# Order and queue assignment of the first loads in a gated mix of linear attention and a GEGLU feed-forward block

## The chip, the cores and the metric

The kernel runs on one core of one Trainium2 chip. The metric is the device time of one execution in microseconds (us); the number compared is the median over several executions of the same program. A profiled execution also has a span, the time from its first to its last instruction.

## The reference

All tensors are bf16; S = 2048 rows, D = 640 columns, F = 1728 hidden columns, 32 heads of 20.

```python
x = A_x                                                 # (1, 2048, 640)
g = sigmoid((x * gate_w).sum(-1, keepdims=True))
q, k, v = split_heads(x @ A_wqkv)                       # A_wqkv (640, 1920)
phi = lambda t: where(t > 0, t + 1, exp(t)) + 1e-6
kv, z = einsum("bhsd,bhse->bhde", phi(k), v), phi(k).sum(s)
o = einsum("bhqd,bhde->bhqe", phi(q), kv) / (einsum("bhqd,bhd->bhq", phi(q), z) + 1e-6)
a = merge_heads(o) @ A_wo
b = (gelu(x @ B_w_gate) * (x @ B_w_up)) @ B_w_down
out = g * a + (1 - g) * b
```

## The kernel before

The program is one long list of operations for five engines. Each operation is recorded by a helper, `P.op`, with the buffers that it reads and writes; from these the helper derives the semaphore waits. Nothing reorders the list: each engine runs its operations in the order in which the source records them, and each DMA queue (SP's, issued by SyncE, and ACT's, issued by ScalarE) gets its loads in that order too. Every load has a semaphore of its own, so whoever needs one chunk waits for that chunk alone.

The 2048 rows are 16 tiles of 128 rows, and the 640 columns of x are 5 chunks of 128 (index k). The work on TensorE goes through these stages, in this order:

1. The start. `warm(count, n)` (line 417) issues matmuls on constants, whose results nobody reads. `T(i, ks, tb)` (line 431) transposes the chunks `ks` of x tile i on TensorE into PSUM bank `tb`, and VectorE copies the result into `xT` (line 435): one copy for chunk 0, one for chunks 1 to 4. This is done for the x tiles 0 and 1 only. `KM(n, [k])` (lines 451 and 452) multiplies chunk k of x tile n by chunk k of the K weights `wk`, 512 and 128 columns, and accumulates over k. `gate_col` puts `gate_w` into column 640 of the Q weights. `QM` (lines 466 and 467) does for the Q weights `wq` what `KM` does for `wk`.
2. `KQ(i)` (line 536) does both products for the x tiles 2 to 15. Their transposed form comes by DMA transposes (line 373) that SP issues; the first of them waits for `wk` chunk 4. ScalarE and VectorE form phi from PSUM (lines 476 to 490, 546 to 555).
3. The products phi(k) with x (lines 593 to 608), the two hidden products of the feed-forward block (line 697), in which the attention's small matrices are formed as well, and the output products (lines 808 to 861).

The first loads, each of 160 KB (128 rows of 640 bf16) apart from two small ones, are recorded in this order; `load_x(i)` loads x tile i, `load_wk(k)` and `load_wq(k)` load the 128 rows of chunk k of the K and of the Q weights:

| Queue | Loads in order |
|---|---|
| SP | x tile 0, wk 0, wk 1, wk 3, wq 0, wq 2, wq 4, then the transposes |
| ACT | touch load, x tile 1, wk 2, wk 4, gate_w (1.2 KB), wq 1, wq 3 |

The touch load (line 355) reads 16 pieces of 8 bytes from the K weights into a buffer that nothing reads. Between x tile 1 and wk 2, ScalarE also has an exp on a constant (line 364), before which its table is loaded.

The start of TensorE's list reads:

```python
warm(5, 512)
warm(1, 128)
T(0, [0], 7)
T(0, [1, 2, 3, 4], 6)
warm(6, 128)
KM(0, [0])
T(1, [0], 7)
T(1, [1, 2, 3, 4], 6)
warm(3, 128)
KM(1, [0])
for k in (1, 2, 3):
    KM(0, [k])
    KM(1, [k])
gate_col()
```

Of the kernel before, what the change touches and what calls it, by code (L numbers as in the profile page):

```python
# [161 lines left out]
def bass_gated_mix__linear_attn_block__geglu_ffn__prompt_kernel(  # L162
# [63 lines left out]
    with (  # L226
# [8 lines left out]
        with contextlib.ExitStack() as stack:  # L235
            dma_sems = [stack.enter_context(nc.semaphore("s_in%d" % i)) for i in range(n_dma_in)]

            P = _Plan(["pe", "act", "dve", "pool", "sp"])
# [9 lines left out]
            def new_dma_key():  # L248
                k = "in%d" % dma_next[0]
                dma_next[0] += 1  # L250
                return k

            def v16(o, n):
                return pool[:, o:o + n]
# [46 lines left out]
            touch = v16(O_TOUCH, 16)  # L301
# [37 lines left out]
            def dma_in(dst, src, writes, reads=(), eng="sp"):  # L339
                P.op(eng, lambda e, dst=dst, src=src: e.dma_start(dst, src),  # L340
                     reads=reads, writes=writes, dma=new_dma_key())
# [3 lines left out]
            def load_x(i, eng="sp"):  # L345
                dma_in(x_aug[:, i, 0:640], A_x[0, i * 128:(i + 1) * 128, :], [r_xn[i]], eng=eng)

            def load_wk(k, eng="sp"):
                dma_in(wk[:, k, :], A_wqkv[k * 128:(k + 1) * 128, 640:1280], [r_wk[k]], eng=eng)

            def load_wq(k, eng="sp"):
                dma_in(wq[:, k, 0:640], A_wqkv[k * 128:(k + 1) * 128, 0:640], [r_wq[k]], eng=eng)


            P.op("act", lambda e: e.dma_start(touch[0:16, 0:4], A_wqkv[0:128:8, 640:644]),
                 writes=[P.res("touch")], dma=new_dma_key())
            load_x(0)
            load_wk(0)
            load_x(1, "act")
            load_wk(1)  # L360
            load_wk(3)

            zero = nc.const_aps.tensor(0.0, (128, 1), F32)
            P.op("act", lambda e: e.activation(eg[:, 0:1], zero, ACT.Exp), writes=[r_eg[0]])
            load_wk(2, "act")
            load_wk(4, "act")
            P.op("dve", lambda e: e.memset(gw_sb, 0.0), writes=[r_gw])
            dma_in(gw_sb[0:5, :], gate_w.rearrange("(k p) -> k p", p=128), [r_gw], eng="act")
            for k in range(KC):
                load_wq(k, ("sp", "act")[k % 2])  # L370

            def load_xT(i, after=()):
                P.op("sp", lambda e: e.dma_start_transpose(xT[:, :, i * 128:(i + 1) * 128],
# [39 lines left out]
            def warm(count, n):  # L413
                def fn(e):
                    last = None
                    for w in range(count):
                        last = e.matmul(ps[:, 4, 0:n], one_l, one_r[:, 0:n], start=True, stop=True)
                    return last
                P.op("pe", fn, writes=[bank[4]])
# [4 lines left out]
            def slot(n):  # L424
                return SLOTS[n % 4]

            def T(i, ks, tb):
                def fn(e):
                    last = None
                    for n, k in enumerate(ks):  # L430
                        last = e.transpose(psb[:, tb, n * 128:(n + 1) * 128],
                                           x_aug[:, i, k * 128:(k + 1) * 128], ident)
                    return last
                P.op("pe", fn, reads=[r_xn[i], r_ident], writes=[bank[tb]])
                P.op("dve", lambda e: e.tensor_copy(
                    xT[:, ks[0]:ks[-1] + 1, i * 128:(i + 1) * 128],
                    psb[:, tb, 0:len(ks) * 128].rearrange("p (k s) -> p k s", k=len(ks))),
                    reads=[bank[tb]], writes=[r_xTa[i] if ks[0] == 0 else r_xT[i]])
# [4 lines left out]
            def KM(n, ks):  # L443
                i = seq[n][1]
                b0, b1 = slot(n)

                def fn(e):
                    last = None
                    for k in ks:
                        lhs = xT[:, k, i * 128:(i + 1) * 128]  # L450
                        e.matmul(ps[:, b0, :], lhs, wk[:, k, 0:512], start=(k == 0), stop=(k == KC - 1))  # L451
                        last = e.matmul(ps[:, b1, 0:128], lhs, wk[:, k, 512:640],
                                        start=(k == 0), stop=(k == KC - 1))
                    return last
                P.op("pe", fn, reads=[r_xTa[i] if i < NXN and ks == [0] else r_xT[i]] + [r_wk[k] for k in ks],
                     writes=[bank[b0], bank[b1]])
# [51 lines left out]
            KM(0, [0])  # L508
            T(1, [0], 7)
            T(1, [1, 2, 3, 4], 6)  # L510
            warm(3, 128)
            KM(1, [0])
            for k in (1, 2, 3):
                KM(0, [k])
                KM(1, [k])
            gate_col()
# [409 lines left out]
```

## Time and profile before

| What | Value |
|---|---|
| Median of 5 runs | 274.27 us (273.56 to 274.69) |
| The profiled execution | 274.07 us, its span 272.8 us |
| TensorE matmuls (PE) | busy 268.6 us, 98% of the span |
| VectorE (DVE) | busy 141.8 us, 52% |
| ScalarE (ACT) | busy 76.0 us, 28% |
| GpSimd (POOL) | busy 30.0 us, 11% |
| DMA | 23.61 MB, 87 GB/s on average |

The engines' busy times overlap, so they don't add up to the span. A matmul's busy time runs from its start until its result has drained, and the next one starts before that; the distance between the starts of two neighbours tells the pace. PEld is the load of the stationary operand. SPq and ACTq are the sequencers of SyncE and ScalarE when they issue a DMA; "us to landing" is the time from the issue until the last piece has arrived and the semaphore is full.

### The profile page before, as it was taken

The page shows a single profiled execution, that of the slowest core. Times are in us where ns is not written, and L with a number is a line of the kernel's source. Part 1 is how long each engine was busy: PE and PEld are TensorE (multiplying, and loading weights), DVE is VectorE, ACT ScalarE, POOL GpSimd, SP SyncE. Part 2 cuts the span into 40 slices and gives each one's busy share as a digit, 9 for nine tenths or more (in the row PEclk, how much of TensorE's full clock was granted, in tenths as well). Part 3 has the DMA queues.
Part 4 walks back from the last instruction along what each step waited for, and adds up shares of the span by engine and source line. Part 5 has one row for each costly group of instructions (what it writes and reads, how often), then busy time and mean ns, then how long its engine had stood idle before and what let it go on. Part 6 is the DMA issues. An engine that isn't in the chain of part 4 may idle for free.

```text
span 272.8 us, 3426 instructions
## 1 busy us (share of the span) xinstructions
PE 268.6 (98%) x1343; PEld 128.8 (47%) x1369; DVE 141.8 (52%) x251; ACT 76.0 (28%) x132; POOL 30.0 (11%) x28
## 2 busy tenths in 40 slices
PE   8999999999999999999999999999999999999997
PEld 4555555544445444444444444444444444444444
DVE  2698988998233335999999999634210000000200
ACT  2455554310422453233222223224011122121021
POOL 5000000003240002242332422000000000000000
DMA  7776999600200011512221221263031110110211
GB/s 224 163 111 123 316 401 388 156 3 16 61 19 2 23 50 50 188 39 48 26 48 24 48 45 30 60 221 103 5 77 38 41 38 19 38 41 19 58 58 41
DMA packets 42208, 23.61 MB, mean 87 GB/s; under 512 B 31567, under 2 KB 40783, under 8 KB 42063
## 3 DMA queue, kind: packets, MB, share of 16 engines
q1 hardware_dynamic: 41429, 22.56, 30.7%
q10 hardware_dynamic: 762, 0.82, 0.9%
q8 instruction: 11, 0.18, 0.3%
q14 instruction: 6, 0.05, 0.1%
HBM read 13.83 MB, written 2.63 MB: 60 GB/s over the span
## 4 chain that ended last, share of the span: by engine, by line
PE 94%; DVE 2%; DMA 2%; issue 1%; ACT 1%; SPq 0%; DVEq 0%; ACTq 0%
PE ps L697 41%; PE ps L861 23%; PE ps L536 12%; PE ps L593 6%; PE ps L840 4%; PE ps L808 2%; DMA pool<-in_A_wqkv_dram 2%; PE ps L675 2%; PE ps L596 2%; PE ps L821 1%; PE ps L451 1%; PE ps L466 1%; DVE pool L490 1%; PE ps L718 1%; DVE pool L555 1%
## 5 line engine op out<-in xcount | busy, mean ns | idle before, releaser
L697 PE MATMUL ps<-pool 128*128 128x512 bf16 x510 | 113.0, 379 | 0.5
L697 PEld LDWEIGHTS ps<-pool 128*128 128x128 bf16 x520 | 50.5, 98 | 60.0
L861 PE MATMUL ps<-pool 128*128 128x512 bf16 (+2 forms) x300 | 62.4, 366 | 0.3
L703 ACT ACTIVATE pool<-ps 128x512 f32<-128x512 f32 x52 | 31.1, 597 | 73.1 <-PE ps L697 73.1
L705 DVE TENSOR_TENSOR pool<-ps,pool 128x512 bf16<-128x512 f32 x52 | 34.7, 689 | 31.7 <-PE ps L697 30.4
L861 PEld LDWEIGHTS ps<-pool 128*128 128x128 bf16 x306 | 29.2, 98 | 33.4 <-issue 0.4
L536 PE MATMUL ps<-pool 128*128 128x512 bf16 (+1 forms) x206 | 37.9, 343 | 0.2
L844 DVE TENSOR_TENSOR pool<-ps,pool 128x512 bf16<-128x512 f32 x4 | 2.8, 692 | 61.5 <-PE ps L840 61.5
L751 POOL TENSOR_TENSOR pool<-pool 128x640 f32<-128x640 bf16 x16 | 22.5, 1407 | 72.8 <-DVE pool L753 65.7
L868 ACT ACTIVATE pool<-ps,pool 128x512 bf16<-128x512 f32 (+1 forms) x16 | 10.9, 681 | 68.6 <-PE ps L861 68.6
L536 PEld LDWEIGHTS ps<-pool 128*128 128x128 bf16 x210 | 20.5, 98 | 17.5
L555 DVE SCALAR_TENSOR_TENSOR pool<-ps,pool 128x128 bf16<-128x128 f32 (+2 forms) x42 | 25.3, 602 | 2.4
L546 ACT ACTIVATE pool<-ps 128x640 bf16<-128x640 f32 x28 | 19.7, 704 | 18.1 <-DVE pool L555 10.6
L593 PE MATMUL ps<-pool 128*128 128x512 bf16 x76 | 19.2, 379 | 0.1
L761 DVE TENSOR_TENSOR pool<-pool 128x640 bf16<-128x640 bf16 x16 | 13.2, 825 | 0.6
L759 DVE TENSOR_SCALAR pool<-pool 128x32 f32<-128x32 f32 x16 | 12.9, 804 | 0.6
L753 DVE TENSOR_REDUCE pool<-pool 128x32 f32<-128x640 f32 x16 | 12.9, 809 | 0.0
L641 DVE TENSOR_TENSOR pool<-pool 128x640 f32<-128x640 f32 x14 | 11.6, 825 | 0.5
L840 PE MATMUL ps<-pool 128*128 128x512 bf16 x51 | 11.5, 379 | 0.1
L643 POOL PARTITION_ALL_REDUCE pool<-pool x1 | 4.0, 3972 | 61.3 <-DVE pool L641 61.3
L593 PEld LDWEIGHTS ps<-pool 128*128 128x128 bf16 x78 | 7.0, 98 | 7.2
L552 DVE TENSOR_SCALAR pool<-pool 128x640 bf16<-128x640 bf16 x28 | 9.1, 327 | 1.8 <-ACT pool L546 0.4
(70 smaller groups left out, 106.4 us busy)
## 6 DMA issues: line engine op xcount, KB each, us to landing
out_dram<-pool SPq DMA_DIRECT2D x19, 128.0 KB, 1.7
pool<-in_B_w_gate_dram SPq DMA_DIRECT2D x1, 2080.0 KB, 14.5
pool<-in_B_w_up_dram SPq DMA_DIRECT2D x1, 2080.0 KB, 19.1
pool<-in_A_x_dram SPq DMA_DIRECT2D x1, 1280.0 KB, 8.7
pool<-in_B_w_down_dram SPq DMA_DIRECT2D x1, 1120.0 KB, 6.1
pool<-omg_row SPq DMA_DIRECT2D x1, 1024.0 KB, 4.6
pool<-in_A_wqkv_dram SPq DMA_DIRECT2D x6, 160.0 KB, 4.7
pool<-in_A_x_dram SPq DMA_DIRECT2D x1, 960.0 KB, 5.5
```

The costliest lines, as they stand in the source:

```text
L536: last = e.matmul(ps[:, b + p, 0:c1 - c0], xT[:, k, i * 128:(i + 1) * 128], wkq[:, k, c0:c1], start=(k == 0), stop=(k == KC - 1))
L546: P.op("act", lambda e: e.activation(e_buf[m], ps_flat[:, o:o + 640], ACT.Exp), reads=banks, writes=[r_e[m]])
L555: P.op("dve", lambda e, c0=c0, c1=c1: e.scalar_tensor_tensor(dst[:, c0:c1], ps_flat[:, o + c0:o + c1], 1.0 + EPS, e_buf[m][:, c0:c1], ALU. ...
L593: last = e.matmul(ps[:, b, :], pk[i][:, c * 128:(c + 1) * 128], x_aug[:, i, 0:512], start=(i == 0), stop=(i == NT - 1))
L697: last = e.matmul(ps[:, b, :], w[:, k, fc * 128:(fc + 1) * 128], xT[:, k, j * 512:(j + 1) * 512], start=(k == 0), stop=(k == KC - 1))
L703: P.op("act", lambda e: e.activation(ge[n], ps[:, gb, :], ACT.Gelu_apprx_tanh), reads=[bank[gb]], writes=[r_ge[n]])
L705: P.op("dve", lambda e: e.tensor_tensor(hT[fc][:, j * 512:(j + 1) * 512], ps[:, ub, :], ge[n], ALU.mult), reads=[bank[ub], r_ge[n]], write ...
L751: P.op("pool", lambda e: e.tensor_tensor(tmp[n], pq[i], z_b, ALU.mult), reads=[r_pq[i], r_zb], writes=[r_tmp[n]])
L753: P.op("dve", lambda e: e.tensor_reduce(den[n], tmp[n].rearrange("p (h d) -> p h d", h=32), AX.X, ALU.add), reads=[r_tmp[n]], writes=[r_de ...
L761: P.op("dve", lambda e: e.tensor_tensor(pq[i].rearrange("p (h d) -> p h d", h=32), pq[i].rearrange("p (h d) -> p h d", h=32), den[n].unsqu ...
L840: last = e.matmul(ps[:, b, :], wd[:, fc, 512:640], hT[fc][:, j * 512:(j + 1) * 512], start=False, stop=(fc == NFC - 2), skip_group_check=True)
L861: last = e.matmul(ps[:, pb, 0:c1 - c0], lhs, rhs, start=False, stop=(q == len(rows) - 1), skip_group_check=True)
```

## The change

The queues' lists become:

| Queue | Loads in order |
|---|---|
| SP | x tile 0, x tile 1, wk 2, wk 4, wq 1, wq 3, then the transposes |
| ACT | wk 0, wk 1, wk 3, gate_w, wq 0, wq 2, wq 4 |

The touch load is dropped. On ScalarE the exp on a constant stands between wk 1 and wk 3. On TensorE, `warm(3, 128)` is dropped, and `KM(0, [1])` stands in its place, ahead of `KM(1, [0])`; `KM(1, [1])` follows it. Nothing else changes on any engine.

```diff
-            P.op("act", lambda e: e.dma_start(touch[0:16, 0:4], A_wqkv[0:128:8, 640:644]),
-                 writes=[P.res("touch")], dma=new_dma_key())
             load_x(0)
-            load_wk(0)
-            load_x(1, "act")
-            load_wk(1)
-            load_wk(3)
+            load_wk(0, "act")
+            load_x(1)
+            load_wk(1, "act")
+            load_wk(2)
+            load_wk(4)
 
             zero = nc.const_aps.tensor(0.0, (128, 1), F32)
             P.op("act", lambda e: e.activation(eg[:, 0:1], zero, ACT.Exp), writes=[r_eg[0]])
-            load_wk(2, "act")
-            load_wk(4, "act")
+            load_wk(3, "act")
             P.op("dve", lambda e: e.memset(gw_sb, 0.0), writes=[r_gw])
             dma_in(gw_sb[0:5, :], gate_w.rearrange("(k p) -> k p", p=128), [r_gw], eng="act")
             for k in range(KC):
-                load_wq(k, ("sp", "act")[k % 2])
+                load_wq(k, ("act", "sp")[k % 2])
...
             T(1, [1, 2, 3, 4], 6)
-            warm(3, 128)
+            KM(0, [1])
             KM(1, [0])
-            for k in (1, 2, 3):
+            KM(1, [1])
+            for k in (2, 3):
                 KM(0, [k])
                 KM(1, [k])
```

## The prediction

> **What bounds the kernel now.** I read the page's busy shares first: TensorE is busy for 98% of the span. The chain of waits, in order of time and up to 12 us, then says what TensorE waits for at the start:
>
> ```profile
> 0.79 0.40 SPq L340
> ...
> 1.26 0.41 SPq L340
> ...
> 1.71 4.31 DMA pool<-in_A_wqkv_dram
> 6.01 0.05 issue
> 6.06 0.39 PE ps L451
> ```
>
> The chain runs through SP's third load, wk 1: issued at 1.71, landed at 6.01 us. `KM(0, [1])` starts 0.05 later, and from there to the last matmul the chain is nearly all TensorE. The neighbours' starts show no pause longer than 0.1 us after 6.06 that isn't one missing matmul record (0.22 us). So the time of the kernel is the moment at which the dense stretch begins, plus a constant. A move of that moment by 0.1 us moves the whole time by 0.1 us.
>
> The timeline from 4.7 to 6.7 us shows what stands just ahead (start, duration, engine, line):
>
> ```profile
> 4.29 0.63 PE L451 MATMUL ps<-pool 128*128 128x512 bf16 x1
> 4.72 0.31 PE L452 MATMUL ps<-pool 128*128 128x128 bf16 x1
> ...
> 4.83 0.69 PE L431 MATMUL ps<-pool 128*128 128x128 bf16 x5
> ...
> 5.35 0.34 PE L417 MATMUL ps<-const-bfloat16-1.0 128*128 128x128 bf16 x3
> ...
> 5.53 0.38 PE L451 MATMUL ps<-pool 128*128 128x512 bf16 x1
> ...
> 5.55 0.42 DVE L435 COPY pool<-ps 128x512 bf16<-128x512 bf16 x1 [0.15 <-PE ps L431]
> 5.74 0.22 PE L452 MATMUL ps<-pool 128*128 128x128 bf16 x1
> 6.06 0.10 PEld L451 LDWEIGHTS ps<-pool 128*128 128x128 bf16 x1 [0.43 <-DMA pool<-in_A_wqkv_dram]
> ```
>
> Two things are to be seen. First, there are 0.18 us of dummies (5.35 to 5.53) and, after the last pair, some 0.26 us of nothing (5.80 to 6.06: at this pace a 128-column matmul takes 0.06). Second, TensorE's pace changes. At 4.29 a 512-column matmul holds the array for 0.43 us (next start 4.72), at 5.53 for 0.21 us: the pace doubles at about 5.3 us, 4.5 us after the first matmul (0.82). The granted clock reads 1.00 in every window of the profile, so here the distances of starts are the evidence, not that column.
>
> The windows say whether the loads are limited by latency or by bandwidth (busy of each engine, then granted clock, DMA share, GB/s):
>
> ```profile
> 0.82:3.14 2.32, 2.31 (x6) 0.70 (x7) 0.11 (x1) 1.42 (x2) 1.96 (x4) 1.00 0.47 129
> 3.14:5.25 2.11, 2.11 (x18) 1.83 (x18) 0.72 (x3) 0.07 (x1) 1.37 (x4) 1.00 1.00 314
> 5.25:6.06 0.81, 0.71 (x8) 0.38 (x7) 0.57 (x2) 0.00 (x0) 0.00 (x0) 1.00 1.05 368
> ```
>
> From 3.14 on the DMA engines are full. With 129 GB/s for 2.32 us and 314 for 2.11, some 960 KB, nearly six loads, have been moved by 5.25, yet only three had landed: the end of wk 1 trails. The DMA issues, asked for one by one, give the first landings (KB, us to landing):
>
> ```profile
> pool<-in_A_wqkv_dram ACTq DMA_DIRECT2D x1, 0.1 KB, 2.1
> pool<-in_A_x_dram SPq DMA_DIRECT2D x1, 160.0 KB, 2.3
> pool<-in_A_x_dram ACTq DMA_DIRECT2D x1, 160.0 KB, 3.1
> pool<-in_A_wqkv_dram SPq DMA_DIRECT2D x1, 160.0 KB, 2.8
> pool<-in_A_wqkv_dram SPq DMA_DIRECT2D x1, 160.0 KB, 4.3
> ```
>
> Added to their issues (0.78, 0.79, 1.23, 1.26, 1.71): the touch load landed at 2.9, x tile 0 at 3.1, x tile 1 at 4.3, wk 0 at 4.0, wk 1 at 6.0 us. The next ones were wk 2 at 6.2, wk 3 at 6.8, wk 4 at 7.1.
>
> **The change, part by part.**
>
> *The touch load goes.* It cost ACT's queue one issue slot, 0.45 us (0.78 to 1.23), and moved 0.1 KB. Every later ACT load is issued 0.45 us earlier. Nothing waited for it.
>
> *wk 0 at ACT's head* is issued at 0.78 instead of 1.26. It is needed by `KM(0, [0])`, which in the trace started at 4.29, right behind the six dummies, with wk 0 there at 4.0. So its earlier landing is worth nothing. Its price is what it takes from x tile 0, which now shares the DMA engines. At best nothing is lost: a load of 0.1 KB took 2.1 us and x tile 0 took 2.3, so it is nearly all latency. At worst wk 0's 160 KB are interleaved evenly, 160 KB at 314 GB/s, which makes 0.5 us. I take 0.1, nearer to the latency row, because ACT's first large load took 0.8 us longer than SP's first, so that wk 0 should start behind x tile 0 rather than beside it. TensorE waits for x tile 0 (`T(0)` began at 3.14, its dummies having ended at 3.02), so the delay, call it d, moves all that follows.
>
> The Trainium skill, "DMA: Bandwidth & Descriptors" (Rules for kernel authors), speaks against the change: spreading loads over several issuing engines buys no bandwidth, since all run on the same 16 DMA engines and interleave. Taken to the letter it would make d the even share, 0.5 us, and the sum below would be a loss of 0.2 us rather than a gain.
>
> *x tile 1 moves to SP's second place*, issued at 1.26 instead of 1.23. It is needed at 4.83+d and landed at 4.3 on the queue that starts later; hidden, with 0.5 us of cover.
>
> *wk 1 moves to ACT's second place*, issued at 1.23 instead of 1.71. By bytes, four loads have been moved when 655 KB have: 300 KB at 3.14, the rest at 314 GB/s, at 4.3; landing trails by 0.4 (x tile 0 to 1 show as much), so 4.7 us. By the queue, ACT's second large load landed at 6.2 and would now stand 0.45 earlier, 5.8. I take 5.3, in the middle.
>
> *`warm(3, 128)` goes and `KM(0, [1])` stands there.* After `T(1)` TensorE can run `KM(0, [1])` at 5.35+d and `KM(1, [0])` at 5.63+d (0.28 us a pair, by the starts 6.06, 6.34 and 6.62 of the next ones). `KM(1, [1])` needs VectorE's second copy of `T(1)`, which ended at 5.55+0.42=5.97; with 0.05 for the signal, as behind the load, it starts at 6.02+d. Before, it started at 6.34. So the new wait that replaces the load is this copy, and the dense stretch gains 0.32−d=0.22 us if wk 1 is there by 5.4. If it lands at 5.8, `KM(0, [1])` starts at 5.85, `KM(1, [1])` at 6.41: a loss of 0.07. What is queued behind these waits is all of TensorE's list, so either counts in full.
>
> *The chunks behind.* At 0.22 earlier, wk 2 is needed at 6.40, wk 3 at 6.95, wk 4 at 7.5, the first Q chunk at 8.05 and one more each 0.55 us (four matmuls of two pairs at the new pace). The queues' bytes are the same without the touch load, so I keep the landings of equal positions: wk 2 (SP's third) 6.0, wk 3 (ACT's third) 7.1−0.45=6.6, wk 4 (SP's fourth) 6.8: in time, with 0.35 to 0.7 us of cover. The first Q chunk moves to ACT's fourth place (before 8.4, now some 7.9): the tightest, 0.15 us of cover, and a wait of 0 to 0.3 us if that is gone. The transposes wait for wk 4, which lands no later. gate_w is issued 0.45 us earlier. On ScalarE the exp keeps its place ahead of the first real one at 8.20, idle for 5.0 us before it.
>
> *The sum.* Gain 0.32 (0.18 dummies, 0.26 of wait, less 0.12 of new wait for the copy), less 0.1 for x tile 0: 0.2 us. The span becomes 272.6 and the profiled execution 273.9 instead of 274.07. The median of the runs stood 0.2 above that execution; it becomes 274.1. With the unknown terms at their ends it is 273.95 (d=0) to 274.6 (d=0.5, which turns the gain into a loss of 0.2, and 0.1 of waiting for the Q chunk). What a measurement of this kernel can tell from no change is about 0.3%, 0.8 us, so "faster" starts under 273.45 and "slower" over 275.09.
>
> **The rivals.**
>
> *The pace of TensorE doubles later (slower).* In the trace the dummies and the first real work ran with a hole of only 0.12 us (3.02 to 3.14) before the doubling. With d the hole grows to 0.2 to 0.6. If that breaks the stretch which must be unbroken, the 4.5 us count from `T(0)` at 3.3, and the doubling moves from 5.3 to 7.8: 2.5 us at half pace lose 1.2, less the 0.3 that no longer wait for loads, so 275.2. It decides from the hole on that the clock counts as idleness, which no row shows; for it speaks only that the dummies are cut to fit the landing. Against it: 0.12 us did no harm, and a hole of 0.5 is a tenth of the stretch. The Trainium skill, "TensorE: Matmul & The Clock Gate" (Part 1), says that the gate opens after a busy window of about 3.4 us which runs freely, not from the kernel's start. By it a missed window would cost half of 3.4, 1.7 us, 275.7; and the moment differs from run to run anyway.
>
> *More is gained than this execution shows (faster).* The runs spread over 1.1 us and the median is 0.2 above the profiled one, the slowest 0.6. If that spread is the trailing end of wk 1, two places further back in the stream than it will be, the change removes it as well: 0.2 and 0.3 to 0.6 more, 273.4.
>
> *wk 1 lands no earlier (no effect).* Landings are by bandwidth and not by the order of issue; the last piece of wk 1 trails by the same, 5.8, and the median stays at 274.3.
>
> *Both heads share evenly.* d=0.5: a loss of 0.2, 274.5.
>
> **How the numbers follow.** The forecast gets 0.50, the later doubling 0.18, the larger gain 0.14, no effect 0.12, even sharing 0.06. Of the forecast 0.03 fall out on either side by the runs' spread. Faster: 0.12 of the larger gain and 0.03, 0.15. Slower: 0.18 and 0.03, 0.21. Within 0.3%: the rest, 0.64. The range goes from the larger gain's value to just past the later doubling's, 273.4 to 275.3, and leaves out about half of each of these two; the likeliest case's own range is 273.95 to 274.6.
>
> **What would show it.** In the new profile `T(0)` starts between 3.14 and 3.3, and no L417 row follows `T(1)`. The first pause after that is ended by VectorE's copy, not by a load, and the pair of `KM(1, [1])` starts near 6.1. The distance of starts doubles its pace near 5.3. wk 1 lands before 5.5. I am wrong if 512-column matmuls still stand 0.43 us apart after 6 us, if `T(0)` begins after 3.6, or if a Q chunk is waited for.

## The result and the profile after

The changed kernel takes 275.4 us (median of 28 runs, 273.73 to 276.3), the kernel before 274.23 us (49 runs, 273.47 to 275.2). The ratio is 1.0038, with a 95% interval of 1.0028 to 1.0048: slower by 1.2 us at the median. The forecast was 274.1, the upper end of the range 275.3.

The profiled execution took 276.14 us, its span 274.9 against 272.8. It is among the slowest of the 28, so it shows a loss of 2.1 us where the median loses 1.2. The chain of waits up to 12 us, for the changed kernel, begins:

```profile
0.79 3.19 DMA pool<-in_A_x_dram
3.98 0.05 issue
4.02 0.71 PE ps L429 x5
4.74 0.64 PE ps L415 x6
5.38 0.43 PE ps L449
```

Where the kernel before had wk 1 in this chain, there is now x tile 0. It lands at 3.98 us, 3.19 after its issue, where it took 2.3. From 4.02 on the chain holds no load and no copy, only TensorE. The timeline shows what TensorE does there (start, duration, engine, line; the dummies had ended at 3.02):

```profile
4.02 0.71 PE L429 MATMUL ps<-pool 128*128 128x128 bf16 x5 [0.80 <-DMA pool<-in_A_x_dram]
...
6.24 0.63 PE L449 MATMUL ps<-pool 128*128 128x512 bf16 x1
...
6.67 0.31 PE L450 MATMUL ps<-pool 128*128 128x128 bf16 x1
...
8.90 0.63 PE L449 MATMUL ps<-pool 128*128 128x512 bf16 x1
...
9.33 0.31 PE L450 MATMUL ps<-pool 128*128 128x128 bf16 x1
...
9.44 0.45 PE L449 MATMUL ps<-pool 128*128 128x512 bf16 x1
...
9.81 0.38 PE L449 MATMUL ps<-pool 128*128 128x512 bf16 x1
```

At 8.90 a 512-column matmul still holds the array for 0.43 us. The pace doubles between 9.44 and 9.81; the trace's clock record (an entry that gives the time from which a granted clock holds) puts it at 9.58. Before, it doubled at 5.3. The 4.3 us of additional half pace cost 2.15 us, and the span is 2.1 us longer; by this reckoning the lateness of `T(0)`, 0.88 us of which half counts while the pace is half, is about made up by the dummies and the wait for wk 1 that are gone. The last matmul starts at 272.79 against 270.71 us.

The windows over the first packets, before (first pair) and after (second pair; the last two columns are the share and GB/s of the DMA engines), show how x tile 0 comes to be late:

```profile
1.80:2.60 0.80, 0.80 (x4) 0.26 (x2) 0.00 (x0) 0.80 (x1) 0.73 (x2) 1.00 0.71 203
2.60:3.40 0.80, 0.80 (x6) 0.29 (x5) 0.00 (x0) 0.60 (x2) 0.73 (x2) 1.00 0.95 286
```

```profile
1.80:2.60 0.80, 0.80 (x4) 0.26 (x2) 0.00 (x0) 0.80 (x1) 0.73 (x2) 1.00 0.65 126
2.60:3.40 0.80, 0.62 (x3) 0.03 (x1) 0.00 (x0) 0.58 (x2) 0.73 (x2) 1.00 1.04 373
```

With wk 0 at ACT's head the engines do not move 314 GB/s to be shared but 126, less than the 203 of before, when the touch load stood there. Single packets took up to 0.80 us in this stretch, up to 0.35 before, although the median packet took 0.055 in both. By the packet records ACT's first came at 1.82 us and SP's at 2.05, and x tile 0 got 32 of the 126 GB/s. So it got well under half of a slow start.

That is not so with any two large heads. In the experiment below in which x tile 1 stands at ACT's head, 283 GB/s were moved in the same stretch, and x tile 0 landed only 0.43 us later than before:

```profile
1.80:2.60 0.80, 0.80 (x4) 0.27 (x2) 0.00 (x0) 0.79 (x2) 0.73 (x2) 1.00 0.91 283
```

In all four profiles in which x tile 0 and wk 0 are the two heads the rate there was 107 to 133 GB/s.

### The profile page after: what moved, and what is told of

It reads as the page before. It is cut to its first block, busy times and chain, and to the rows that moved or that the text cites. A ratio compares the mean times of both kernels' runs of the same rounds, so it can differ in the third digit from the quotient of the medians.

```text
span 274.9 us, 3419 instructions
## 1 busy us (share of the span) xinstructions
PE 270.0 (98%) x1340; PEld 129.4 (47%) x1366; DVE 141.8 (52%) x251; ACT 76.0 (28%) x132; POOL 30.0 (11%) x28
## 4 chain that ended last, share of the span: by engine, by line
PE 97%; DMA 1%; issue 1%; DVE 0%
PE ps L696 41%; PE ps L860 23%; PE ps L535 14%; PE ps L592 6%; PE ps L839 4%; PE ps L807 2%; PE ps L674 2%; PE ps L595 1%; PE ps L449 1%; DMA pool<-in_A_x_dram 1%; PE ps L820 1%; PE ps L464 1%; PE ps L717 1%; PE ps L429 0%; PE ps L735 0%
```

## The experiments

The theory after this profile: the large load at ACT's head makes x tile 0 late; that opens a hole in TensorE's stream; and the hole, more than the lateness, costs the time, by putting off the doubling. The rivals: the lateness itself; the new order of TensorE's list; the order or the number of bytes of the other loads. All medians below stand against runs of the kernel before on the same chip; the changed kernel was not run again beside them, so its 275.4 is that of the result.

**The hole filled.** The changed kernel with

```diff
-            warm(1, 128)
+            warm(10, 128)
```

> The changed kernel, with nine more 128-column dummies ahead of T(0) (warm(10, 128) for warm(1, 128)), so that the dummies end at about 3.98 us, where x tile 0 landed in the changed kernel's profile, and not at 3.02. Hole theory (the idle hole of 1.0 us before T(0) puts off the doubling of TensorE's pace): x tile 0 lands as late as before, but the pace doubles some 2 us earlier on average; the median falls by 0.8 to 1.2, to 274.2 to 274.6. Direct theory (T(0)'s 0.9 us of lateness is the loss, dummies do nothing): 275.4, no change.

274.46 us against 274.22; ratio 1.001 (1.000 to 1.002). Some 0.9 of the 1.2 us come back although nothing but dummies was added. In the profiled execution (the slowest of its twelve, 274.83 us) x tile 0 landed later still, at 5.15, yet the span is 273.6:

```profile
0.82 3.14 PE L415 MATMUL ps<-const-bfloat16-1.0 128*128 128x512 bf16 x15 [0.82 <-PEq L910]
5.20 0.45 PE L429 MATMUL ps<-pool 128*128 128x128 bf16 x5 [1.23 <-DMA pool<-in_A_x_dram]
5.49 0.51 PE L415 MATMUL ps<-const-bfloat16-1.0 128*128 128x128 bf16 x6
5.84 0.38 PE L449 MATMUL ps<-pool 128*128 128x512 bf16 x1
6.05 0.22 PE L450 MATMUL ps<-pool 128*128 128x128 bf16 x1
```

At 5.84 the 512-column matmul holds the array for 0.21 us: the pace had doubled inside the dummies, at about 3.6. `T(0)` began 1.2 us later than in the changed kernel's profile, and the end came 1.3 us earlier. The direct theory fails.

**The hole alone.** The kernel before with

```diff
-            warm(5, 512)
+            warm(3, 512)
```

> The kernel before, loads untouched, with two 512-column dummies fewer ahead of T(0) (warm(3, 512) for warm(5, 512)). They end at about 2.17 us and x tile 0 still lands at 3.1: a hole of 0.97 us, as large as in the changed kernel, with no load moved. Hole theory: T(0) still starts near 3.14, yet the pace doubles later, and the median rises from 274.2 by 0.6 to 1.0, to 274.8 to 275.2. Direct theory: dummies compute nothing and nothing that they precede starts later, so 274.2, no change.

275.42 us against 274.22; ratio 1.0046 (1.0033 to 1.0059). No load is moved, x tile 0 lands at 3.11, and two dummies fewer cost what the change cost. Its timeline:

```profile
3.16 0.71 PE L431 MATMUL ps<-pool 128*128 128x128 bf16 x5 [0.78 <-DMA pool<-in_A_x_dram]
...
7.75 0.63 PE L451 MATMUL ps<-pool 128*128 128x512 bf16 x1
8.18 0.31 PE L452 MATMUL ps<-pool 128*128 128x128 bf16 x1
8.29 0.55 PE L451 MATMUL ps<-pool 128*128 128x512 bf16 x1
8.68 0.22 PE L452 MATMUL ps<-pool 128*128 128x128 bf16 x1
8.73 0.38 PE L451 MATMUL ps<-pool 128*128 128x512 bf16 x1
8.95 0.22 PE L452 MATMUL ps<-pool 128*128 128x128 bf16 x1
```

`T(0)` starts as before (3.16), and the pace doubles at 8.6 instead of 5.3 (a 512-column matmul holds the array for 0.43 us at 7.75 and for 0.22 at 8.73). In this execution a wait of 0.5 us for wk 0, which landed at 4.67, came on top of the hole of 0.99. I had put the loss a little lower, at 0.6 to 1.0.

**The loads without the list.** The changed kernel with TensorE's list of before:

```diff
-            KM(0, [1])
+            warm(3, 128)
             KM(1, [0])
-            KM(1, [1])
-            for k in (2, 3):
+            for k in (1, 2, 3):
```

> The changed kernel's loads with TensorE's list of before (warm(3, 128), then KM(1, [0]), then the pairs of k = 1 to 3). If the loads carry the loss: x tile 0 lands near 4.0, the hole stays, the median is 275.4 to 275.7 (the three dummies cost 0.16 to 0.32 again). If the new order of TensorE's list carries it: 274.2.

275.83 us against 274.22; ratio 1.0064 (1.0048 to 1.0079). x tile 0 landed at 4.19. The loads carry the loss. The median lies a little above the 275.4 to 275.7 that I expected.

**The list without the loads.** The kernel before with the diff above reversed:

> The loads of before with the changed kernel's list on TensorE (no warm(3, 128); KM(0, [1]), KM(1, [0]), KM(1, [1])). If the loads carry the loss: x tile 0 lands at 3.1 with no hole before T(0), but KM(0, [1]) waits for wk 1 until about 6.06 with nothing to run from 5.35, so 274.2 to 274.9. If the list carries it: 275.4.

274.06 us against 274.22; ratio 0.9995 (0.9986 to 1.0003): no loss, and no gain that can be told from none. So the new order of the list does not carry the loss. The chain in the profile:

```profile
1.71 3.75 DMA pool<-in_A_wqkv_dram
5.46 0.05 issue
5.51 0.39 PE ps L451
```

wk 1 landed at 5.46 in this execution, 6.01 in the one profiled of the kernel before, with the same loads.

**The touch load back.** The changed kernel with

```diff
+            P.op("act", lambda e: e.dma_start(touch[0:16, 0:4], A_wqkv[0:128:8, 640:644]),
+                 writes=[P.res("touch")], dma=new_dma_key())
             load_x(0)
             load_wk(0, "act")
```

> The changed kernel with the touch load back at the head of ACT's queue, ahead of wk 0; all else as changed. Head theory (a large load at the head of the other queue, issued within 10 ns of x tile 0, shares the DMA engines from the first packet on): wk 0 is issued 0.45 us later, x tile 0 lands at 3.1 to 3.4, the hole before T(0) falls from 1.0 to 0.1 to 0.4 us, and the median is 273.9 to 274.3. Rival (x tile 1 behind x tile 0 on SP, or the bytes in all, make x tile 0 late): 275.4.

274.33 us against 274.17; ratio 1.0021 (0.9994 to 1.0048). x tile 0 landed at 3.05, though x tile 1 still stood behind it on SP: the head theory holds for it. But the twelve times fall into two groups, nine from 273.76 to 274.49 and three from 276.35 to 277.43, which the expectation did not hold; the three make the interval wide. The profiled execution is the slowest, 277.43 us, and shows why. Its timeline from 3 to 11 us, and its windows between the clock records (3.84, 7.25 and 10.67):

```profile
4.86 0.44 PE L431 MATMUL ps<-pool 128*128 128x128 bf16 x5
7.73 0.61 PE L451 MATMUL ps<-pool 128*128 128x512 bf16 x1 [2.43 <-DMA pool<-in_A_wqkv_dram]
8.13 0.31 PE L452 MATMUL ps<-pool 128*128 128x128 bf16 x1
...
10.80 0.38 PE L451 MATMUL ps<-pool 128*128 128x512 bf16 x1
```

```profile
3.84:7.25 3.41, 1.10 (x13) 0.66 (x11) 1.07 (x3) 0.00 (x0) 0.73 (x3) 1.00 0.95 301
7.25:10.67 3.41, 2.94 (x11) 1.42 (x12) 0.00 (x0) 0.00 (x0) 0.00 (x0) 0.50 0.57 179
```

Here the pace had doubled early, at 3.84. Then wk 1 came only at 7.7, TensorE was busy for 1.10 of the 3.41 us, and for the next 3.41 the granted clock (third column from the right) was 0.50. Whether the other two slow executions had the same cause is not shown.

**Before, without the touch load.** The kernel before with

```diff
-            P.op("act", lambda e: e.dma_start(touch[0:16, 0:4], A_wqkv[0:128:8, 640:644]),
-                 writes=[P.res("touch")], dma=new_dma_key())
             load_x(0)
```

> The kernel before without the touch load, all else untouched: x tile 1 then stands at the head of ACT's queue, issued with x tile 0. Head theory: x tile 0 lands near 4 us though the order of the other loads is as before; the hole is some 0.9 us, and the median 275.2 to 275.8. Rival (it is wk 0, which everyone reads first, or the order behind it): 274.2.

275.65 us against 274.17 (5 runs); ratio 1.0058 (1.0040 to 1.0076). With the order of all other loads as before, x tile 1 at ACT's head makes x tile 0 land at 3.53 and TensorE stand still for 0.56 us, and later for another 0.24 until wk 0 came:

```profile
0.79 2.75 DMA pool<-in_A_x_dram
3.53 0.05 issue
3.58 0.71 PE ps L429 x5
```

I had expected x tile 0 near 4 and a hole of 0.9 us. The profiled execution was the fastest of the five, so its own loss is small; how late x tile 0 came in the others is not shown, and the verdict goes by the median.

**The heads swapped.** The changed kernel with

```diff
-            load_x(0)
-            load_wk(0, "act")
+            load_x(0, "act")
+            load_wk(0)
```

> The changed kernel with the heads swapped: x tile 0 at ACT's head, wk 0 at SP's. In the changed kernel ACT's head was issued 6 ns ahead of SP's and its first packet came at 1.82 us, SP's at 2.05. If the first come takes the engines, x tile 0 now lands some 0.2 us earlier than wk 0, at 3.6 to 3.8, and the median is 274.8 to 275.3. If both are simply shared, 275.4 as before.

274.78 us against 274.17; ratio 1.0024 (1.0011 to 1.0038). x tile 0 landed at 3.69, wk 0 at 3.88; ACT's first packet came at 1.81, SP's at 2.21. ACT's head was served first in all five profiles with two large heads: its first packet came at 1.80 to 1.82 us, SP's at 2.00 to 2.31.

**ACT's head held back without a touch load**, wk 0 waiting for a memset:

```diff
+            P.op("pool", lambda e: e.memset(ones32, 1.0), writes=[r_ones])
             load_x(0)
-            load_wk(0, "act")
+            dma_in(wk[:, 0, :], A_wqkv[0:128, 640:1280], [r_wk[0]], reads=[r_ones], eng="act")
...
-            P.op("pool", lambda e: e.memset(ones32, 1.0), writes=[r_ones])
```

> The changed kernel without a touch load, but wk 0 waits for GpSimd's first 128-column memset, so that ACT's head is issued at about 1.1 us and not at 0.785; SP's list is untouched. Timing theory (x tile 0 needs a head start, and whatever fills ACT's first slot gives it): x tile 0 lands at 3.1 to 3.5, the median is 273.9 to 274.6. Warming theory (the touch load prepares ACT's queue or the weights' addresses, time apart): x tile 0 lands near 4, 275.4.

274.45 us against 274.17; ratio 1.0006 (0.9996 to 1.0017). wk 0 was issued at 1.02, x tile 0 landed at 3.50. A quarter of a microsecond of head start undoes most of the loss at the median, though nothing is read ahead of time from the weights. x tile 0 still landed 0.4 us later than before; whether the touch load does more than give twice that head start is not shown.

**How large a hole.** The kernel before with

```diff
-            warm(5, 512)
+            warm(4, 512)
```

> The kernel before, loads untouched, with one 512-column dummy fewer ahead of T(0) (warm(4, 512) for warm(5, 512)): a hole of 0.55 us, where two fewer made 0.99 us and cost 1.2 us. The pace doubled after a window of 3.41 us with 0.7 us of idleness in one profile and did not after one with 1.0 us. Threshold theory (some 0.7 to 1.0 us of idleness in a window are let pass): 274.2 to 274.7, a third of the loss or less. Proportional theory (each 0.1 us of hole costs the same): half the loss, 274.8.

273.99 us against 273.99; ratio 0.9994 (0.9972 to 1.0016). Half the hole cost nothing that these runs can tell, though the interval is wide. The profiled execution is the slowest of the eleven, 275.36 us: in it a wait of 0.43 us for wk 0 came on top of the hole of 0.51.

The kernel with ACT's head held back, with

```diff
-            warm(1, 128)
+            warm(5, 128)
```

> The kernel whose wk 0 waits for GpSimd's memset, with four more 128-column dummies (warm(5, 128) for warm(1, 128)), which end at about 3.45 us, where its x tile 0 landed. Threshold theory: its hole of 0.5 us cost little, so little comes back: 274.2 to 274.5 against 274.45. Proportional theory: 0.5 us come back, 273.9 to 274.0, faster than the kernel before.

274.48 us against 273.99; ratio 1.0015 (0.9998 to 1.0032). Filling a hole of 0.5 us gave nothing back: the ratio was 1.0006 with the hole, on another chip. Both speak against a price proportional to the hole. The profiles say more exactly where it decides. The clock records above stand 3.41 us apart. Taking the 3.41 us that end with the doubling, and the 3.41 before them, TensorE's idle time (its first matmul starts at 0.82) was as in the table. Here a matmul counts only as long as it holds the array at the pace of the moment, not until its result has drained as in the profile's busy time.

| Profile | Doubling at | Idle in the window that ends there | Idle in the one before it |
|---|---|---|---|
| before | 5.3 | 0.13 | mostly ahead of the first matmul |
| hole filled | 3.6 | 0.64 | the same |
| heads swapped | 4.84 | 0.71 | the same |
| before, no touch load | 5.96 | 0.80 | the same |
| half a hole | 8.22 | 0.0 | 0.94 |
| changed kernel | 9.58 | 0.0 | 1.01 |
| hole alone | 8.63 | 0.0 | 1.5 |

So a window with up to 0.80 us of idleness opened the clock and one with 0.94 did not. The other five profiles fit: the windows that opened held 0.07 to 0.69 us, and the two more that stayed closed after the first matmul (new loads with the old list, ACT's head held back) held 1.22, of which 0.7 to 0.8 lay ahead of that matmul. Each row is one execution, and where the trace has no clock record the doubling is read from the matmuls' starts, to about 0.1 us.

## Why the prediction was wrong

**What bounds the kernel** held in part. TensorE is still the bound, but the time is not the start of the dense stretch plus a constant: that stretch began at 4.02 us instead of 6.06, and the span still grew by 2.1. The "constant" holds the moment at which the pace doubles, which the sum left at 5.3. **The chunks behind** were in time, with less need than I worked out, since at half pace they are wanted later; wk 4 landed at 7.58, not by the 6.8 that I had kept, and the transposes started 0.5 us later for it (7.60 against 7.07), but TensorE did not wait. wk 1 landed at 4.46, before the 5.3 of the prediction.

**The price of wk 0 at ACT's head** is the step that failed first; the second is that the sum left the doubling of the pace where it was. The prediction took d=0.1 with a worst case of 0.5; it was 0.88 (3.98 against 3.10), 1.1 in the profile of the new loads with the old list and 2.05 in that of the filled hole. The worst case divided 160 KB by 314 GB/s, a rate from 3.14 us on, but the packets in question move from 1.8 on, where the two heads together got 126 GB/s. Where 283 GB/s were moved, with x tile 1 at ACT's head, the lateness was 0.43, near the even share. And the reason for choosing the lower end, that ACT's first large load is slow to start, read the row wrongly: that load was the second on its queue. As the head of ACT's queue, wk 0 was served ahead of SP's x tile 0 and landed at 3.74. The even share, which the prediction read out of the Trainium skill, "DMA: Bandwidth & Descriptors" (Rules for kernel authors), pointed the right way and still gave too little for wk 0.

**The touch load** was priced as one issue slot for which nobody waited. At the median it was worth 1.1 us in the changed kernel (275.4 without it, 274.33 with it) and 1.5 us in the kernel before (275.65 and 274.17): those 0.45 us were x tile 0's head start. That another delay of ACT's head does most of the same speaks for this.

**The later doubling** was named as the slower rival, with the right mechanism, at a chance of 0.18. That its 275.2 lies so near the measured 275.4 is in part luck: it had the doubling 2.5 us later, the profile 4.3, and the median is taken over executions that differ by 2.6 us. It got that little because it was judged at a hole of 0.2 to 0.6 us, which by the last two experiments costs little indeed. The hole was 1.0. Its count of 4.5 us from `T(0)` was wrong: it took 5.6 in the profile and 1.1 with the heads swapped (3.73 to 4.84), so the doubling is not timed from `T(0)`. The Trainium skill, "TensorE: Matmul & The Clock Gate" (Part 1), has the window at 3413 ns and running freely; the clock records at 3.84, 7.25 and 10.67 us agree with it. The same page (Why this matters for your kernels) advises against idle gaps over some 3 us between bursts. Here less was enough: in the run with the touch load back a pause of 2.43 us took the pace back, while one of 1.23 us after the doubling did not with the hole filled. Before the doubling 1.0 us was enough to put it off.

**The gain of the list**, 0.3 less d, came to 0.16 in the experiment with the loads of before, not distinguishable from nothing. **The larger gain** did not show. Two of the three signs of being wrong came: matmuls 0.43 us apart after 6 us, and `T(0)` after 3.6. **Where the 1.2 us went**, then: about 0.9 into the hole (it comes back when dummies fill it), the rest, about 0.2, probably into lateness that the list does not make up. What stays open is why x tile 0 and wk 0 together start so slowly, and x tile 0 and x tile 1 do not; the packets show it, and no run here tells the cause.

## What to carry to other kernels

The first load that the bounding engine needs should have the DMA engines to itself for a few tenths of a microsecond; here a tiny load, or a wait, at the head of the other queue bought that. Price a load that moves to a queue's head by the rate of the first packets, not by the rate reached later. Dummies that warm TensorE should last until the load has landed, in its late executions too, or until the pace has doubled: before the doubling a hole was nearly free up to a point and put the doubling off by a whole window beyond it.

## What the runs showed of the hardware

With x tile 0 and wk 0 issued within 10 ns as the two heads, the first 0.8 us moved 126 GB/s, against 203 with the touch load in place of wk 0 and 283 with x tile 1 in place of it. In a window of 3.41 us, 0.80 us of idleness did not keep TensorE's clock low and 0.94 did. Once it was up, a window in which TensorE was busy for 2.18 us kept it (the filled kernel, 3.60 to 7.01) and one with 1.10 us did not (the touch load back, 3.84 to 7.25). Transposes counted as work: before the change the window that opened the clock held about 1 us of them, with 0.13 idle; had they counted as idle, it would have been idle for 1.1. One load's last piece can trail its others by more than a microsecond (x tile 0 in the filled kernel: first piece at 3.58, last at 5.15), and TensorE waits for that one.
